# A chunked linear-attention recurrence on TensorE: state with keys on partitions, a 40-column solve, blocks inverted 16 wide and merged

## The chip, the cores and the metric

The kernel runs on one core of a Trainium2 chip. The core has TensorE (PE in the profile; its weight loads are listed apart as PEld), VectorE (DVE), ScalarE (ACT), GpSimd (POOL) and SyncE (SP), each with its own instruction queue worked in order, and 16 DMA engines that they share. The metric is the device time of one execution in microseconds, the median of several runs.

## The reference, cut to what matters

Two parts follow each other. The first is a recurrence over 768 tokens for 4 x 8 heads of width 40 (`S` in the code is the 40 x 40 state of a head):

```python
for t in range(S):
    y[:, :, t] = einsum('bhd,bhde->bhe', rt, state)
    Sa = einsum('bhde,bhe->bhd', state, at)
    state = state * wt[:, :, None, :] - einsum('bhd,bhe->bhde', Sa, bt)
    state = state + einsum('bhd,bhe->bhde', vt, kt)
```

The second is a gated mixture block over the heads' outputs `x` (768 tokens x 320):

```python
h = maximum(x @ w_in, 0)                 # 320 -> 1024
u, v = h[..., :512], h[..., 512:]
v_n = (v - mean(v)) / sqrt(var(v) + 1e-6)
v_s = einsum('ts,bsd->btd', w_spatial, v_n) + b_spatial[None, :, None]
out = (u * v_s) @ w_out                  # 512 -> 320
```

## The kernel before, in words

**Chunks.** The recurrence is worked in chunks of C = 64 tokens. A step `s` (there are 24: two pairs of batches, 12 chunks each) takes one chunk of 16 heads: 8 units `n`, each with two heads (`par` 0 and 1) on partitions 0 to 39 and 64 to 103. Within a chunk the dependence of each token on the earlier ones is a unit lower triangular 64 x 64 system. So a step is: run the decays together (two scans on VectorE, `scan1`, `scan2`, and the products `at_mul`, `sl_mul`), form the triangular matrix, invert it, and use the inverse to get all 64 updates at once.

**The inverse.** `lprime` and `lblock` put the two diagonal 32 x 32 blocks of each triangle into `Lc`. `invert(g)` takes the blocks of four chunks (a group `g`, 32 units on 128 partitions) through a 32 x 32 transpose, 30 rounds of substitution on VectorE (a product, L351, into the PSUM tile `itmp`, and a sum, L355), and two transposes back, `XT0` and `X11`. The off-diagonal block is then made on TensorE for each chunk: `b_l21`, `b_zt`, `b_x21`.

**The step's solve.** The state lies with values on partitions (`Mc`). `c_bp` multiplies it by 104 columns at once, 64 of the readout `r` and 40 of the identity; `c_ff` adds the chunk's own terms; `c_xx` applies the inverse `xf`; all three have 104 moving columns and come in two halves (`g` = 0, 1). ScalarE copies each result from PSUM (`c_bp_out`, `c_ff_out`, `c_xx_out`), GpSimd cuts the strictly triangular parts (`strict`, L396). `c_mp` updates the state, `c_y` adds to the output, `y_store` writes it to DRAM (`xs`). `b_lka` and `b_h` make two more 64 x 64 products a chunk; `b_tok` transposes two factors. The decay at a chunk's end goes through DRAM (`scr_store`, `scn_load`) to be spread over the columns of `Mc`.

**The mixture.** 12 units `j` of 128 tokens x 2 batches: load from `xs` (`m_load`), split into a high and a low part so that three products stand for one (`m_split`), four `m_u` and two `m_v` groups of eight matmuls (L742, L697), normalisation (`m_n1` to `m_n3`), results to DRAM. The weights `w_in` are decoded on VectorE and GpSimd (`decode`) in steps 4 to 10. `phase2` then does the spatial product (`spatial`, L173 to L175) and the output projection (`proj`, L193).

**Order.** Within the first phase the order on every queue is a plan written by hand: `at(t, fn, ...)` gives each piece a time in units of steps, the list is sorted, and the pieces are issued in that order. What lies beyond step 24 (the rest of the mixture) and `phase2` is ordered by the compiler's scheduler. The lines that the change touches most are these:

```python
M1, M2, M3, M4 = 0.22, 0.46, 0.65, 0.80
T_DEC, T_MOE = 4.2, 11
slots = [T_MOE + k // 4 + (M1, M2, M3, M4)[k % 4] for k in range(3 * NS)]
t0 = 2.5 if g == 1 else max(4.5, GS * g - 4 + 0.0)      # invert(g) from t0
t1 = GS * g - 1 + 0.70                                  # to t1
t = PREP.get(q, q - 8 + 0.01)                           # scans and products of chunk q
```

An fp32 matmul of this kernel is two TensorE instructions, each with a weight load of its own, so the counts in the profile are twice those in the code; transposes are one.

Of the kernel before, what the change touches and what calls it, by code (L numbers as in the profile page):

```python
# [18 lines left out]
P = 128  # L19
# [10 lines left out]
NR = C + E  # L30
LATE = 2 * C
# [180 lines left out]
def phase1(ctx, tc, early, late, vtok, win, xs, vns, uts, dscr):  # L212
    nc = tc.nc
    NS = early.shape[1]
    CPB = 12
    LO, HI = slice(0, 64), slice(64, 128)
    PR = (LO, HI)
    RR = (slice(0, E), slice(64, 64 + E))
    LV = slice(0, 64 + E)

# [15 lines left out]
    ps_b = pool("ps_b", 1, space=PSUM)  # L236
    ps_i = pool("ps_i", 1, space=PSUM)
# [24 lines left out]


# [30 lines left out]
    def scr_store(s):  # L294
        if s % CPB == 0:
            return
        sv = st["raw", s][2]
        sc = jit.tile([P, NU], F32, name="sc")
        nc.scalar.activation(sc, sv[:, :, 1], AF.Copy)
        for par in range(2):  # L300
            nc.sync.dma_start(out=scr[s, par], in_=sc[RR[par]])

    def at_mul(s, eng, ns=slice(0, NU)):
        Et, at, sl = st["pre", s]
        oth = st["raw", s][1]
        Ev = Et.rearrange("p (n c) -> p n c", c=WSEG)
        eng.tensor_tensor(out=at[:, ns], in0=oth[:, ns, 0], in1=Ev[:, ns, 0:C], op=ALU.mult)

    def sl_mul(s, eng, ns=slice(0, NU)):
        Et, at, sl = st["pre", s]  # L310
        wseg, oth, sv = st["raw", s]
        k = ns.stop - ns.start
        eng.tensor_tensor(  # L313
            out=sl[:, ns], in0=oth[:, ns, 1:],
            in1=sv[:, ns, 2:C + 2].unsqueeze(2).broadcast_to([P, k, 2, C]), op=ALU.mult,
        )

    def lprime(s):
        Et, at, sl = st["pre", s]
        pl = ps_k.tile([P, NU, HB], F32, name="bk")  # L320
        for n in range(NU):
            for blk in range(2):
                for par in range(2):
                    o = (1 - par) * 64 + blk * HB
                    cs = slice(blk * HB, (blk + 1) * HB)
                    nc.tensor.matmul(  # L326
                        pl[o:o + HB, n, :], lhsT=sl[PR[par], n, par, cs], rhs=at[PR[par], n, cs],
                        start=True, stop=True,
                    )
        st["pl", s] = pl  # L330

    def lblock(s):
        if s % GS == 0:
            st["Lc", s // GS] = inv.tile([P, GS * NU, HB], F32, name="Lc")
        Lc = st["Lc", s // GS]
        u0 = (s % GS) * NU
        nc.vector.tensor_tensor(
            out=Lc[:, u0:u0 + NU, :], in0=st.pop(("pl", s)),
            in1=maskl.unsqueeze(1).broadcast_to([P, NU, HB]), op=ALU.mult,
        )  # L340

    def invert(g):
        Lc = st.pop(("Lc", g))
        A = inv.tile([P, HB, HB], F32, name="A")
        nc.vector.transpose(out=A, in_=Lc.rearrange("p u t -> p t u"))
        yield
        nc.vector.memset(A.rearrange("p t s -> p (t s)")[:, 0:HB * HB:HB + 1], 1.0)
        for k in range(1, HB - 1):
            m = HB - 1 - k
            tp = ps_i.tile([P, m, k], F32, name="itmp")  # L350
            nc.vector.tensor_tensor(  # L351
                out=tp, in0=A[:, k + 1:, k:k + 1].broadcast_to([P, m, k]),
                in1=A[:, k:k + 1, 0:k].broadcast_to([P, m, k]), op=ALU.mult,
            )
            nc.vector.tensor_tensor(out=A[:, k + 1:, 0:k], in0=A[:, k + 1:, 0:k], in1=tp, op=ALU.add)  # L355
            yield
        XT0 = xinv.tile([P, GS * NU, HB], F32, name="XT0")
        X11 = xinv.tile([P, GS * NU, HB], F32, name="X11")
        st["X", g] = (XT0, X11)
        nc.vector.transpose(out=XT0.rearrange("p u t -> p t u"), in_=A)  # L360
        yield
        nc.vector.transpose(out=X11.rearrange("p u t -> p t u"), in_=A.rearrange("p t s -> p s t"))
        yield

    INV_N = HB + 1


    def lin_load(s):
        for par in range(2):
            nc.sync.dma_start(out=lin[s % 2][RR[par], :, 0:LATE], in_=late[par, s])  # L370

    def vtok_load(s):
        for par in range(2):
            nc.sync.dma_start(out=Rts[s % 2][par][PR[1 - par], :, C:], in_=vtok[s, par])

    def b_copy(s, par):
        if par == 0:
            At = [jat.tile([P, NU, C], F32, name=f"At{i}") for i in range(2)]
            tk = jit.tile([P, NU, 2, E], F32, name="tk")
            st["blk", s] = (At, Rts[s % 2], tk, xfs[s % 2])  # L380
# [617 lines left out]
```

## Time and profile before

| | us |
|---|---|
| three runs | 712.87, 704.87, 713.06 |
| median | 712.87 |
| span of the profiled execution | 704.4 |
| TensorE busy (matmuls) | 585.0 (83%) |
| TensorE weight loads | 529.8 (75%) |
| VectorE busy | 447.6 (64%) |
| ScalarE busy | 413.5 (59%) |
| GpSimd busy | 291.1 (41%) |

The profile is of one execution, whose time is its span and about half a microsecond around it if it is like the fastest run; no time of its own is listed for it. Rows of the timeline give the start of a run of like instructions in microseconds from the span's start, the time from its first start to its last end, the engine, the line of the kernel, the operation, the tiles (output <- input), the shape (for PE: rows*loaded columns, then partitions x moving columns) and the count. Rows of groups end in total busy time and mean nanoseconds of one, then the idle time before them and what ended it. Matmuls are pipelined: the length of one in the profile (200 to 400 ns) is its latency, and the distance between starts is what it costs.

### The profile page before, as it was taken

The page shows a single profiled execution, that of the slowest core. Times are in us where ns is not written, and L with a number is a line of the kernel's source. Part 1 is how long each engine was busy: PE and PEld are TensorE (multiplying, and loading weights), DVE is VectorE, ACT ScalarE, POOL GpSimd, SP SyncE. Part 2 cuts the span into 40 slices and gives each one's busy share as a digit, 9 for nine tenths or more (in the row PEclk, how much of TensorE's full clock was granted, in tenths as well). Part 3 has the DMA queues.
Part 4 walks back from the last instruction along what each step waited for, and adds up shares of the span by engine and source line. Part 5 has one row for each costly group of instructions (what it writes and reads, how often), then busy time and mean ns, then how long its engine had stood idle before and what let it go on. Part 6 is the DMA issues. An engine that isn't in the chain of part 4 may idle for free. (4 is left out here: it accounts for less than half of the span.)

```text
span 704.4 us, 25450 instructions
## 1 busy us (share of the span) xinstructions
PE 585.0 (83%) x10784; PEld 529.8 (75%) x10784; DVE 447.6 (64%) x884; ACT 413.5 (59%) x904; POOL 291.1 (41%) x486
## 2 busy tenths in 40 slices
PE   1706975577876778998998999999999989999997
PEld 1605865566766767987886788778889989999997
DVE  7897889977999999867789366612127521332221
ACT  2315773376555677696887789899855443331112
POOL 5101330123334455253563434545448972562221
PEclk9965897589787887799999899999999999999999
DMA  8462775284454635554547335344336464650001
GB/s 184 79 110 47 131 150 115 47 173 83 104 102 106 130 66 124 114 136 96 115 124 227 94 120 133 106 128 122 92 108 185 143 179 139 188 177 29 29 29 57
DMA packets 101337, 81.35 MB, mean 115 GB/s; under 512 B 33576, under 2 KB 90152, under 8 KB 99304
## 3 DMA queue, kind: packets, MB, share of 16 engines
q1 hardware_dynamic: 100680, 78.01, 44.7%
q10 hardware_dynamic: 544, 1.72, 1.2%
q8 instruction: 85, 1.39, 0.9%
q14 instruction: 28, 0.23, 0.1%
HBM read 59.20 MB, written 20.50 MB: 113 GB/s over the span
## 5 line engine op out<-in xcount | busy, mean ns | idle before, releaser
L396 POOL TENSOR_SCALAR_AFFINE_SELECT Rt<-Rt 64x512 f32<-64x512 f32 (+1 forms) x144 | 83.1, 579 | 97.1 <-ACT Rt L582 69.5
L545 ACT ACTIVATE Rt<-bp 64x416 f32<-64x416 f32 x96 | 49.1, 511 | 67.5 <-PE bp L535 65.8
L396 POOL TENSOR_SCALAR_AFFINE_SELECT At<-At 64x512 f32<-64x512 f32 x48 | 38.4, 801 | 93.5 <-ACT At L406 91.3
L351 DVE TENSOR_TENSOR itmp<-A 128x30 f32<-128x30 f32 (+9 forms) x180 | 74.7, 415 | 3.2
L173 PE MATMUL pg<-wsh,vh 128*128 128x384 f32 x192 | 64.8, 337 | 0.0
L174 PE MATMUL pg<-wsl,vh 128*128 128x384 f32 x192 | 64.7, 337 | 0.0
L175 PE MATMUL pg<-wsh,vl 128*128 128x384 f32 x192 | 64.6, 337 | 0.0
L355 DVE TENSOR_TENSOR A<-A,itmp 128x30 f32<-128x30 f32 (+9 forms) x180 | 59.0, 328 | 6.2
L535 PE MATMUL bp<-lin,Mc 40*64 40x104 f32 x768 | 51.6, 297 | 10.7 <-DVE y L640 10.2
L177 DVE TENSOR_TENSOR g<-pg,bb 128x384 f32<-128x384 f32 x32 | 17.8, 555 | 63.5 <-PE pg L175 58.5
L535 PEld LDWEIGHTS bp<-lin,Mc 40*64 40x64 f32 x768 | 45.2, 164 | 14.7 <-DVE y L640 12.6
L54 POOL TENSOR_TENSOR gl<-g,gh 128x384 fp32r<-128x384 f32 x32 | 33.2, 1041 | 51.1 <-ACT gh L50 50.9
L582 ACT ACTIVATE Rt<-ch 64x416 f32<-64x416 f32 x96 | 49.1, 511 | 3.9 <-PE ch L571 1.5
L326 PE MATMUL bk<-at,sl 64*32 64x32 f32 x1536 | 23.6, 215 | 30.3 <-DVE sl L313 15.2
L553 PE MATMUL ch<-Rt,At 128*64 128x104 f32 x768 | 44.9, 271 | 1.2 <-issue 1.2
L441 PE MATMUL bk<-ident,sl 128*128 128x128 f32 x192 | 31.5, 298 | 16.9 <-ACT At L406 6.8
L50 ACT ACTIVATE gh<-g 128x384 fp32r<-128x384 f32 x32 | 16.6, 522 | 48.7 <-DVE g L178 48.7
L326 PEld LDWEIGHTS bk<-at,sl 64*32 64x32 f32 x1536 | 19.7, 127 | 33.2 <-DVE sl L313 15.3
L705 DVE BATCH_NORM_STATS2 bs<-vr 128x6 f32<-128x512 f32 x24 | 16.6, 690 | 42.9 <-ACT vr L699 42.9
L571 PE MATMUL ch<-ffs,xf 64*64 64x104 f32 x768 | 43.1, 263 | 0.3 <-issue 0.3
L553 PEld LDWEIGHTS ch<-Rt,At 128*64 128x64 f32 x768 | 39.1, 147 | 5.7 <-issue 3.1
L54 POOL TENSOR_TENSOR vl<-raw,vh 128x512 fp32r<-128x512 f32 x24 | 32.1, 1348 | 25.5 <-ACT vh L50 20.6
(135 smaller groups left out, 1597.3 us busy)
## 6 DMA issues: line engine op xcount, KB each, us to landing
ein<-in_early SPq DMA_DIRECT2D x40, 387.0 KB
lin<-in_late SPq DMA_DIRECT2D x48, 160.0 KB
uts<-ur SPq DMA_DIRECT2D x48, 128.0 KB
vns<-vr SPq DMA_DIRECT2D x24, 256.0 KB
raw<-vns SPq DMA_DIRECT2D x24, 256.0 KB
ut<-uts SPq DMA_DIRECT2D x24, 256.0 KB
Rt<-in_vtok SPq DMA_DIRECT2D x48, 80.0 KB
xs<-y SPq DMA_DIRECT2D x48, 80.0 KB
```

Of the source, the lines that this page charges most:

```text
L54: eng.tensor_tensor(out=lo, in0=x, in1=hi.bitcast(F32), op=ALU.subtract)
L173: nc.tensor.matmul(pg, lhsT=vh[:, dc], rhs=w_h, start=(i == 0), stop=False)
L174: nc.tensor.matmul(pg, lhsT=vh[:, dc], rhs=w_l, start=False, stop=False)
L175: nc.tensor.matmul(pg, lhsT=vl[:, dc], rhs=w_h, start=False, stop=(i == NT - 1))
L326: nc.tensor.matmul(pl[o:o + HB, n, :], lhsT=sl[PR[par], n, par, cs], rhs=at[PR[par], n, cs], start=True, stop=True,)
L351: nc.vector.tensor_tensor(out=tp, in0=A[:, k + 1:, k:k + 1].broadcast_to([P, m, k]), in1=A[:, k:k + 1, 0:k].broadcast_to([P, m, k]), op=AL ...
L355: nc.vector.tensor_tensor(out=A[:, k + 1:, 0:k], in0=A[:, k + 1:, 0:k], in1=tp, op=ALU.add)
L396: nc.gpsimd.affine_select(out=t, in_=t, pattern=[[0, k], [1, C]], base=0, channel_multiplier=-1, compare_op=ALU.is_gt, fill=0.0,)
L535: nc.tensor.matmul(bp[PR[par], q, :], lhsT=Mc[RR[par], n, :], rhs=li[RR[par], n, C:], start=(q == 0), stop=False, skip_group_check=True,)
L545: nc.scalar.activation(Rt[par][PR[par], gp, :], st["bp", g][PR[par]], AF.Copy)
L553: nc.tensor.matmul(ff[PR[1 - par], q, :], lhsT=At[par][:, n, :], rhs=Rt[par][:, n, :], start=True, stop=True,)
L582: nc.scalar.activation(Rt[par][PR[par], gp], xx[PR[1 - par]], AF.Copy, scale=-1.0)
```

## The change

The state is kept with keys on partitions (`St`) and the solve has 40 moving columns in place of 104. `c_fv` and `c_ff` add up the right side of the solve, `c_u` applies the inverse twice, once in each orientation (`u`: tokens on partitions; and its transpose into `uvr`), `c_mp` updates `St`. The output comes from two parts: `c_ys` multiplies the state (transposed by `c_sd` into `Sd`) by `r`, and `c_gh` and `c_y` add the chunk's own terms. `c_y` runs in the next step.

`low` makes both strictly lower products of a chunk at once, with 128 loaded columns, in place of `lprime`, `b_lka` and `b_l21`. `invert` runs the substitution on 16 x 16 blocks (14 rounds, two blocks in one instruction, `itmp` in SBUF), and TensorE merges 16 to 32 (`b_y`, `b_xx`) and 32 to 64 (`b_w`, `b_x21`) for every chunk. The scans of a group's four chunks run in the first step and a half of the group before, the inversion from 1.6 to 3.2. The mixture starts at 7.4 steps in place of 11.2, the weight decode at 1.0 in place of 4.2. The decay stays on the chip (`dec_copy`).

The diff, cut to its core:

```diff
+    DEPTH = 7
+    SB = HB // 2
-    jat = pool("jat", 2)
-    linp = pool("linp")
-    etp = pool("etp", 9)
+    slp = pool("slp", 2)
+    etp = pool("etp", 8)
+    uvr = const.tile([P, NU, 4, C], F32, name="uvr")
+    itmp = const.tile([P, P], F32, name="itmp")
...
+    def low(s):
+        pt = [ps_k.tile([P, NU, C], F32, name="bk") for par in range(2)]
+        for n in range(NU):
+            for par in range(2):
+                nc.tensor.matmul(
+                    pt[par][:, n, :], lhsT=sl[RR[par], n].rearrange("p q c -> p (q c)"),
+                    rhs=at[RR[par], n, :], start=True, stop=True,
+                )
+    def lblock(s, par, eng=None):
+        for blk in range(2):
+            strict(Lc[rows, us], NU, st["tl", s][par][rows, :, cs], HB)
...
     def invert(g):
+        for k in range(1, SB - 1):
+            m = SB - 1 - k
+            tp = itmp[:, 0:2 * m * k].rearrange("p (b m k) -> p b m k", b=2, k=k)
+            nc.vector.tensor_tensor(out=tp, in0=D[:, :, k + 1:SB, k:k + 1]..., in1=D[:, :, k:k + 1, 0:k]..., op=ALU.mult)
+            nc.vector.tensor_tensor(out=D[...], in0=D[...], in1=tp, op=ALU.subtract)
...
+    def b_y(s):
+        for n in range(NU):
+            for o in range(0, P, HB):
+                nc.tensor.matmul(
+                    m4[o:o + HB, n, :], lhsT=Lc[o:o + HB, u0 + n, :], rhs=X11[o:o + HB, u0 + n, 0:SB], ...)
+    def b_xx(s):
+        for n in range(NU):
+            for o in range(0, P, HB):
+                nc.tensor.matmul(m5[o:o + HB, 0, n, :], lhsT=wy[o:o + HB, n, :], rhs=XT0[o:o + HB, u0 + n, SB:], ...)
+        for n in range(NU):
+            for o in (0, 64):
+                nc.tensor.matmul(m5[o:o + HB, 1, n, :], lhsT=XT0[o:o + HB, u0 + n, :], rhs=wy[o:o + HB, n, 0:SB], ...)
+            for o in (0, 64):
+                nc.tensor.matmul(m5[o:o + HB, 1, n, :], lhsT=ident[...], rhs=X11[o:o + HB, u0 + n, 0:SB], ...)
+    def b_w(s):
+                nc.tensor.matmul(m2[o:o + 64, n, :], lhsT=tl[par][o:o + HB, n, :], rhs=X11[o:o + HB, u0 + n, :], ...)
     def b_x21(s):
+                nc.tensor.matmul(m3[o:o + 64, n, :], lhsT=wi[o + HB:o + 64, n, :], rhs=XT0[o + HB:o + 64, u0 + n, :], ...)
     def b_xcopy(s):
+            nc.sync.dma_start(out=xfs[s % 2][o:o + HB, :, 0:HB], in_=XT0[o:o + HB, us])
...
+    def c_fv(s, g):
+                nc.tensor.matmul(ff[PR[1 - par], q, :], lhsT=tl[par][PR[par], n, :], rhs=Rt[par][PR[par], n, :], ...)
     def c_ff(s, g):
+                nc.tensor.matmul(st["ff", g][PR[1 - par], q, :], lhsT=at[RR[par], n, :], rhs=Sv[RR[par], n, :], ...)
+    def c_u(s, g):
+                nc.tensor.matmul(u[PR[par], q, 0:E], lhsT=xf[ev, n, :], rhs=ffs[ev, q * E:(q + 1) * E], ...)
+                nc.tensor.matmul(u[PR[par], q, E:], lhsT=ffs[ev, q * E:q * E + C], rhs=xf[ev, n, :], ...)
     def c_mp(s, g):
+                nc.tensor.matmul(st["ff", g][RR[par], q, :], lhsT=tk[:, n, par, :], rhs=Rt[par][:, n, :], ...)
+    def c_sd(s):
+                nc.tensor.matmul(sd[PR[par], n, :], lhsT=St[RR[par], n * E:n * E + C], rhs=ident[RR[par], RR[par]], ...)
+    def c_ys(s):
+                nc.tensor.matmul(yb[PR[par], n, :], lhsT=Sd[RR[par], n * E:n * E + C], rhs=uvr[RR[par], n, 3, :], ...)
+    def c_gh(s):
+                nc.tensor.matmul(gh[par][:, n, :], lhsT=uvr[RR[par], n, par:2 + par, :]..., rhs=uvr[RR[par], n, 3, :], ...)
     def c_y(s):
+                nc.tensor.matmul(yb[RR[par], n, :], lhsT=tk[:, n, par, :], rhs=ghs[par][:, n, :], ...)
...
+            at(s + 0.00 + 0.02 * g, c_fv, s, g)
+            at(s + 0.01 + 0.02 * g, c_ff, s, g)
+            at(s + 0.20 + 0.05 * g, c_u, s, g)
+            at(s + 0.36 + 0.05 * g, c_mp, s, g)
+        at(s + 0.06, c_sd, s)
+        at(s + 0.62, c_ys, s)
+        at(s + 0.50, c_gh, s)
+        ty = s + (1.12 if s < NS - 1 else 0.80)
+        at(ty, c_y, s)
+        at(b + 0.30, b_y, q)
+        at(b + 0.46, b_xx, q)
+        at(b + 0.47, b_xcopy, q)
+        at(b + 0.64, b_w, q)
+        at(b + 0.76, b_x21, q)
+        at(b + 0.64, uvr_load, q)
+    PREP = (0.05, 0.40, 0.75, 1.10)
+        t = GS * (q // GS) - GS + PREP[q % GS]
+        t0 = GS * g - GS + PREP[3] + 0.50
+        t1 = GS * g - 0.80
+    T_DEC, T_MOE, D_DEC = 1.0, 7.4, 0.9
+        t0 = max(2 * j + 3.28, T_MOE + 1.5 * j)
+        gap = 1 / 3 if t0 + 2 < NS else 0.2
```

More of the change, by code (lines that the diff above doesn't have):

```diff
@@ L292, in scan2, with dec_copy, at_mul @@
         )
-    def scr_store(s):
+    def dec_copy(s):
         if s % CPB == 0:
             return
[L297 to L303, printed above, removed]
+        dec = etp.tile([P, NU], F32, name="dec")
+        act_copy(dec, st["raw", s][2][:, :, 1])
+        st["dk", s] = dec
+    def at_mul(s):
         Et, at, sl = st["pre", s]
@@ L332, in lblock @@
[L332 to L380, printed above, removed]
-        at = st["pre", s][1]
-        nc.scalar.activation(st["blk", s][0][par][PR[par]], at[PR[par]], AF.Copy)
@@ L384, in b_lka @@
-    def b_lka(s):
-        Et, at, sl = st["pre", s]
-        pk = ps_k.tile([P, NU, C], F32, name="bk")
+        pt = [ps_k.tile([P, NU, C], F32, name="bk") for par in range(2)]
         for n in range(NU):
@@ new lines, in vtok_load @@
+    def vtok_load(s):
+        for par in range(2):
+            nc.sync.dma_start(out=Rts[s % 2][par][PR[par]], in_=vtok[s, par])
+    def b_w(s):
+        XT0, X11 = st["X", s // GS]
+        u0 = (s % GS) * NU
+        tl = st["tl", s]
+        m2 = ps_k.tile([P, NU, HB], F32, name="bk")
+        for n in range(NU):
+            for par in range(2):
+                o = 64 - 64 * par
+                nc.tensor.matmul(
+                    m2[o:o + 64, n, :], lhsT=tl[par][o:o + HB, n, :],
+                    rhs=X11[o:o + HB, u0 + n, :], start=True, stop=True,
@@ new lines, in c_gh_out, with c_y @@
+    def c_gh_out(s, par):
+        if par == 0:
+            st["ghs", s] = [jit.tile([P, NU, C], F32, name=f"ghs{i}") for i in range(2)]
+        act_copy(st["ghs", s][par], st["gh", s][par])
+        for rows in PR:
+            strict(st["ghs", s][par][rows], NU)
+    def c_y(s):
+        tk, ghs, yb = st["tk", s], st["ghs", s], st["yb", s]
+        for n in range(NU):
+            for par in range(2):
+                nc.tensor.matmul(
+                    yb[RR[par], n, :], lhsT=tk[:, n, par, :], rhs=ghs[par][:, n, :],
+                    start=(first(s) and n == 0), stop=True, skip_group_check=True,
+                )
@@ L634, in c_y_out @@
+    def c_y_out(s):
         c = s % CPB
```

617 lines of the change are left out of this document (289 added, 328 removed).

## The prediction

> **What bounds the kernel now.** I read the page's engine shares and 40 slices first, then busy time by stage (columns: stretch; its length; PE, PEld, DVE, ACT, POOL busy us; granted clock).
>
> ```profile
> span 704.4 us, 25450 instructions
> ...
> PE   1706975577876778998998999999999989999997
> ...
> DVE  7897889977999999867789366612127521332221
> ```
>
> ```profile
> 74.10:284.00 209.90, 154.45 (x4214) 138.56 (x4204) 191.09 (x361) 129.88 (x289) 76.34 (x94) 0.83 0.54 111
> 284.00:518.40 234.40, 219.44 (x4653) 190.12 (x4641) 136.90 (x301) 195.62 (x427) 111.69 (x223) 0.97 0.45 122
> 518.40:704.40 186.00, 179.51 (x1162) 172.79 (x1160) 59.81 (x113) 63.48 (x134) 86.00 (x131) 1.00 0.37 116
> ```
>
> Three regimes. Up to about 284 us VectorE is the bound (191 of 210 us busy; the granted clock is only 0.83, as PE waits). From 284 PE is (219 of 234), and still in the tail (180 of 186). So a saving on VectorE pays only in the first 284 us; whatever the change adds on PE is paid in full after it.
>
> **What a PE block costs.** Timeline rows of warm blocks (start, from first start to last end, count; an fp32 product is two matmuls, two products on separate parts of the array alternate):
>
> ```profile
> 324.26 0.76 PE L326 MATMUL bk<-at,sl 64*32 64x32 f32 x64
> ...
> 421.22 0.63 PE L742 MATMUL pv<-xh,wh 128*128 128x256 f32 x3
> ...
> 422.37 1.09 PE L627 MATMUL bp<-Rt,tk 128*40 128x64 f32 x32
> ```
>
> ```profile
> 426.96 1.65 PE L553 MATMUL ch<-Rt,At 128*64 128x104 f32 x32
> ...
> 428.54 0.66 PE L441 MATMUL bk<-ident,sl 128*128 128x128 f32 x4
> ...
> 429.79 0.95 PE L697 MATMUL pv<-wh,xh 128*128 128x512 f32 x3
> ...
> 431.81 0.70 PE L458 MATMUL bk<-sl,at 64*32 64x32 f32 x32
> ...
> 435.77 1.15 PE L419 MATMUL bk<-lin 40*64 40x64 f32 x32
> 436.85 0.51 PE L603 MATMUL ch<-tk,Rt 128*40 128x40 f32 x16
> ...
> 438.59 0.69 PE L504 MATMUL bk<-zt,X 32*32 32x32 f32 x32 [0.28 <-ACT zt L486]
> ```
>
> The distance from L553 to the next block is 1.58 us, from L419 1.08; with 0.15 of turnover that is 0.089 a pair at 104 moving columns and 0.058 at 64. L419's length then leaves some 0.23 for its last matmul's own latency; taken off the others it gives about 0.03 a pair at 32 columns (L504), 0.037 at 40 (L603) and 0.034 for each four of L326. I use 0.088, 0.059, 0.038, 0.032 and 0.034, with 0.15 turnover per block, and 0.11 for a transpose.
>
> These shapes all have as many loaded columns as moving ones, or fewer. The change turns that round: 64 loaded and 40 moving, 128 and 64, 64 and 32, 32 and 16. So the weight load's own time decides. The same query cut a moment later shows it (PEld; columns as above):
>
> ```profile
> 426.96 0.14 PEld L553 LDWEIGHTS ch<-Rt,At 128*64 128x64 f32 x2
> 426.96 0.20 PEld L553 LDWEIGHTS ch<-Rt,At 128*64 128x64 f32 x4
> 429.76 0.19 PEld L697 LDWEIGHTS pv<-wh,xh 128*128 128x128 f32 x1
> 429.76 0.30 PEld L697 LDWEIGHTS pv<-wh,xh 128*128 128x128 f32 x2
> 429.76 0.54 PEld L697 LDWEIGHTS pv<-wh,xh 128*128 128x128 f32 x3
> 428.54 0.20 PEld L441 LDWEIGHTS bk<-ident,sl 128*128 128x128 f32 x2
> ```
>
> The second load on each of L553's two array parts ends 0.06 after the first (64 columns); L697's second 0.11 after the first (128). The third comes 0.24 later, when a 512-column matmul has let go: one load is held ready, not two. So a pair cannot be faster than its load: I take 0.059 for 64 loaded columns however few move, 0.112 for 128, 0.032 for 32. L441, a transpose, loads 128 columns in 0.06; that is the low end for the 128-column blocks.
>
> **The step, before and after** (PE us).
>
> Before: lprime 0.7; b_lka, b_h and c_y 1.08 each; the three 32-wide blocks 0.65 each; c_bp, c_ff, c_xx 16 x 0.088 + 0.15 = 1.56 each; transposes 1.0; c_mp 0.9. Sum 12.5.
>
> After: low 16 x 0.112 + 0.15 = 1.94; transposes 1.0; b_y 0.7; b_xx 0.58 + 32 x 0.032 + 0.15 = 1.75; b_w and b_x21 (64 loaded) 1.09 each; c_fv and c_ff 32 x 0.059 + 0.3 = 2.19; c_sd 1.09; c_u 2.19; c_mp 0.9; c_gh 1.94; c_ys and c_y 1.09 each. Sum 18.1: the solve is narrower, but its pairs wait for 64-column loads, and b_y, b_xx and the wide blocks are added.
>
> Over the run: low and transposes for 20 chunks (four lie in the start) 20 x 2.96 = 59; merging for 23 chunks 23 x 4.65 = 107; the step itself 24 x 10.5 = 252, less 8 where a batch starts or ends. Together **410 us**.
>
> A rule of the Trainium skill speaks against narrowing as such: "TensorEngine Tiling (Array Packing)", Instruction Overhead, says a matmul of one moving column takes as long as one of 60. The rows disagree (0.032 a pair at 32 columns, 0.059 at 64). By the rule b_y and b_xx would cost an estimated 1.7 us more a step, 38 in all.
>
> Stalls come on top. One late step:
>
> ```profile
> 423.61:441.53 17.92, 16.93 (x360) 14.77 (x360) 11.81 (x29) 16.39 (x35) 8.60 (x17) 1.00 0.49 131
> ```
>
> Its blocks, without lprime 11.8, and three L742 groups (421.22 to 422.37: 1.15) and one L697 group (429.79 to 431.81: 2.02) sum to 17.3, so 0.65 was stall; the stretch 284 to 518 (12 steps, 8 mixture units of 4 x 1.15 + 2 x 2.02 = 8.64) leaves 1.5 a step. I take 1.1: 24 x 1.1 = **26**. The new merge adds two PE-ACT-PE turns a step, but the plan puts other blocks between.
>
> **VectorE.** Rows (last columns: busy us, mean ns):
>
> ```profile
> L351 DVE TENSOR_TENSOR itmp<-A 128x30 f32<-128x30 f32 (+9 forms) x180 | 74.7, 415 | 3.2
> L355 DVE TENSOR_TENSOR A<-A,itmp 128x30 f32<-128x30 f32 (+9 forms) x180 | 59.0, 328 | 6.2
> L345 DVE STREAM_TRANSPOSE A<-Lc 128x1024 f32<-128x1024 f32 x6 | 11.8, 1961 | 0.2
> L281 DVE TENSOR_TENSOR_SCAN S<-ein,ends 128x528 f32<-128x528 f32 x24 | 30.3, 1263 | 1.1 <-DMA ein<-in_early 1.1
> L313 DVE TENSOR_TENSOR sl<-ein,S 128x1024 f32<-128x1024 f32 x24 | 33.7, 1405 | 0.0
> L617 DVE TENSOR_TENSOR Mc<-mn,scn 104x160 f32<-104x160 f32 x44 | 22.4, 508 | 1.4
> L640 DVE TENSOR_TENSOR y<-bp,Et 104x256 f32<-104x256 f32 x48 | 19.9, 419 | 24.0 <-PE bp L627 23.9
> L382 ACT ACTIVATE At<-at 64x512 f32<-64x512 f32 x48 | 30.2, 629 | 0.9
> 0.00:740.00 740.00, 42.33 (x70) 5.65 (x10) 27.24 (x20) 0.91 0.45 110
> ```
>
> Substitution goes from 60 instructions a group (22.3 us) to 28 of 28 to 112 elements; between
>
> ```profile
> 52.28 0.27 DVE L355 TENSOR_TENSOR A<-A,itmp 128x108 f32<-128x108 f32 x1
> ...
> 53.88 0.19 DVE L355 TENSOR_TENSOR A<-A,itmp 128x30 f32<-128x30 f32 x1
> ```
>
> that is about 0.27 each with its gap: 7.6, with three transposes (5.9) and memsets 14 instead of 28. A step then has 5.1 of scans and products (L281, L313 and two between them), 3.5 of inversion, 2.2 of state and output (about two L617, two sums and two L640) and, in steps 1 to 6.4, 5.5 of weight decode (the last row is the decode's tiles over the span: 42.3 us, some 30 of it for these weights): 16.3, below PE's 19.2. So VectorE stops being the bound, and its 14 us a group buy only what PE leaves.
>
> **What is costed at nothing.** ScalarE loses six copies of 64x512 (L382: 0.63) and eight of 64x416, gains fewer and smaller ones, and has spare time in every step; uncovered it would add no more than the two turns above. POOL has ten selects a step instead of eight, needed half a step later; c_y alone waits for the last four, about 3 us, and lies 0.6 of a step behind them. The copy of the diagonal block goes from ScalarE to SP, 0.7 of a step ahead of its reader. One wait is new there: the load of r and v for the next step waits for c_ys of this one, because that tile is single now; behind it on SP stand the output store and the next loads, whose readers are most of a step away. The decay's store and broadcast load leave SP (88 transfers). The mixture's loads and stores move four steps forward past the decode's, into a stretch where the DMA engines are half busy (0.54 in the first stage row). If SP's order did stall PE, it would be a transfer's 2 to 3 us in some steps: under 20 in all, inside the range.
>
> **The start.**
>
> ```profile
> 25.04 1.11 PE L441 MATMUL bk<-ident,sl 128*128 128x128 f32 x4
> ...
> 29.64 1.96 DVE L345 STREAM_TRANSPOSE A<-Lc 128x1024 f32<-128x1024 f32 x1
> ...
> 55.87 1.92 DVE L362 STREAM_TRANSPOSE X<-A 128x1024 f32<-128x1024 f32 x1
> ...
> 62.58 1.06 PE L458 MATMUL bk<-sl,at 64*32 64x32 f32 x32
> 63.58 3.04 PE L571 MATMUL ch<-ffs,xf 64*64 64x104 f32 x32
> ```
>
> The first inversion runs alone, 29.64 to 57.8, and the first solve starts at 63.6. PE is cold here (L458's block 1.06, not 0.70). Per chunk PE now has low (about 3.3 cold), two transpose blocks of 1.1 and evictions between, some 6.6 us against VectorE's 5.1, so the fourth chunk's blocks reach POOL late and the inversion starts near 37. It takes 14, and then four merges in series, cold, about 10: **61** to the first solve (54 if PE warms, 66 if not). Of the 14 us saved, some 3 remain.
>
> **Sum.** 61 + 410 + 26 + mixture 12 x 8.64 = 104 + second phase 147 (the last stretch's 186, less 4 units, 35, and 5 for the rest of a step) + 2 for the seam, where spatial weights now wait for buffers of steps 21 to 23: **750** against the profiled 704.4. Starting the mixture at step 7 moves PE work forward into a PE-bound stretch: nothing is gained. The three runs were 704.87, 712.87 and 713.06; the profiled one agrees with the fastest, so against the median 712.9 this is +5%. One measurement cannot tell 2% (14 us) from no change.
>
> **Rivals.**
> 1. *Loads stay hidden*: pairs go by moving columns. low, c_gh 1.09; b_w, b_x21 0.66; c_fv with c_ff 1.5; c_sd 0.76; c_u 1.85: 14.3 a step, 322 in all, 88 less; VectorE's 16.3 then binds in steps 1 to 6, +7: **669**, clearly faster. Against it: one load is held ready. For it: no row has more loaded than moving columns. It decides if a 64/40 pair takes under 0.05. Chance 0.12.
> 2. *Only 128-column loads are quick* (0.06, as L441's): low and c_gh 1.09: 750 - 44 x 0.85 = **713**. Chance 0.07.
> 3. *Row halves don't run side by side*: low and c_gh use rows 0-39 and 64-103 but all 128 columns; no row shows that. If serial, 32 x 0.107: +1.6 for each of 44 blocks: **822**. Chance 0.12. The Trainium skill, "TensorE: Matmul & The Clock Gate", The mechanism, says loads overlap running matmuls only when row groups differ, which low and c_gh meet; by it the sum stays 750. L553's rows disagree in part: its loads overlap with all 128 rows in use.
> 4. *Queue stalls*: ps_k turns nine tiles a step through two buffers, PE waits on ACT 2 us a step: 772. Within the forecast's own spread of 725 to 775.
>
> **Numbers.** Forecast 0.66 (its lower tail to 725), rivals 1 to 3 0.31, others 0.03. Range 705 to 822: it leaves out rival 1 and half of rival 3. Faster by over 2% (below 698.6): rival 1 and a bit, 0.15. Within 2% (to 727): rival 2 and the forecast's edge, 0.14. Slower 0.71.
>
> **What would show it.** PE 95% busy in all steps, VectorE below 85% before 200 us; steps near 19 us without mixture and 25 with it; blocks of 32 with 64 loaded and 40 moving columns 1.1 long, those of low and c_gh 2.0; the first solve near 61. If c_fv's 16 matmuls take 0.5 from start to end instead of 0.7, rival 1 holds and I am wrong.

## The result: 931.4 us, 1.32 times the time before

The changed kernel takes a median of 931.43 us (929.42 to 942.86, four runs) beside 709.85 for the kernel before (704.87 to 713.06): a ratio of 1.317, 95% interval 1.307 to 1.327. The forecast was 750, range 705 to 822: the sign is right, the size is not. The profiled execution took 929.42, its span 927.7.

From the page of the changed kernel (engine totals, then slices; PEclk is the granted clock in tenths):

```profile
span 927.7 us, 33760 instructions
...
PE 850.1 (92%) x15200; PEld 788.6 (85%) x15200; DVE 344.1 (37%) x646; ACT 298.6 (32%) x760; POOL 338.6 (36%) x534
...
PE   4579799999999998999999999999999787999998
...
DVE  7444515464442522243523244523111431423221
...
PEclk9999856756566685778877779667977697999999
```

And by stage (stretch; length; busy time of PE, PEld, DVE, ACT, POOL; granted clock; DMA share, GB/s), with the first stretch of the kernel before and the totals of its page ahead:

```profile
0.00:74.10 74.10, 31.58 (x796) 28.29 (x800) 59.82 (x110) 24.51 (x55) 17.04 (x38) 0.78 0.56 106
```

```profile
PE 585.0 (83%) x10784; PEld 529.8 (75%) x10784; DVE 447.6 (64%) x884; ACT 413.5 (59%) x904; POOL 291.1 (41%) x486
```

```profile
0.00:74.10 74.10, 45.91 (x738) 42.23 (x740) 42.57 (x71) 18.11 (x47) 28.20 (x48) 1.00 0.49 97
74.10:284.00 209.90, 196.56 (x4194) 184.66 (x4192) 97.77 (x180) 60.72 (x167) 72.37 (x92) 0.68 0.31 68
284.00:518.40 234.40, 226.20 (x4550) 204.76 (x4550) 81.59 (x161) 83.29 (x221) 86.58 (x154) 0.74 0.35 83
518.40:766.00 247.60, 228.25 (x4842) 204.98 (x4830) 79.84 (x165) 90.17 (x235) 82.17 (x170) 0.77 0.32 89
766.00:927.70 161.70, 153.21 (x912) 151.99 (x912) 42.33 (x70) 46.31 (x92) 69.25 (x72) 0.96 0.33 104
```

VectorE went from 191 busy microseconds in the second stretch to 98, and PE from 154 to 197 of 210: PE is the bound from step 1 on, as forecast. What was not forecast stands in the clock column: 0.68, 0.74 and 0.77 where PE is 92 to 97% busy. Every clock record is 0.5 or 1.0, so a mean of 0.74 over 234 us is 2 x 0.26 x 234 = 122 us at half clock. Over the run the records give 379 us at half clock, before the change 126. (The first record is at 103.8 us, before the change at 34.0; until then the page shows 1.00, but the pitches are those of half clock. The half-clock times of the runs below are those of the records alone. The first record comes at 19 to 103.8 us, depending on the run, so small differences between these times mean little.)

The 223 us between the two spans can be split. PE's busy time (the time in which the trace has a matmul running), with half weight where the records say 0.5 and before the first of them, is its work at full clock: 531 us before, 636 after. The rest of its busy time is lost to the clock: 54 before, 214 after. What is left of the span is PE's idle time: 119 and 78. So 223 = **104 of work, 161 of clock, 42 less idle**. With the clock loss of before, and all else equal, the span would have been 767.

### The profile page after: what moved, and what is told of

Read it like the earlier page. It is cut to its first block, busy times and chain, and to the rows that moved or that the text cites. A ratio compares the mean times of both kernels' runs of the same rounds, so it can differ in the third digit from the quotient of the medians.

```text
span 927.7 us, 33760 instructions
## 1 busy us (share of the span) xinstructions
PE 850.1 (92%) x15200; PEld 788.6 (85%) x15200; DVE 344.1 (37%) x646; ACT 298.6 (32%) x760; POOL 338.6 (36%) x534
## 4 chain that ended last, share of the span: by engine, by line
PE 88%; issue 3%; ACT 3%; DMA 2%; DVE 2%; SPq 1%; POOL 0%; ACTq 0%; DVEq 0%; POOLq 0%
PE bk L328 7%; PE pv L713 7%; PE ch L625 7%; PE pv L758 6%; PE po L191 5%; PE bk L495 4%; PE bk L363 4%; PE ff L517 4%; PE bk L474 4%; PE yb L643 4%; PE pg L171 4%; PE pg L172 4%; PE pg L173 4%; PE yb L616 4%; PE ch L545 3%
## 5 line engine op out<-in xcount | busy, mean ns | idle before, releaser
L340 POOL TENSOR_SCALAR_AFFINE_SELECT Lc<-tl 32x256 f32<-32x256 f32 x96 | 62.4, 650 | 148.7 <-ACT tl L270 136.1
L340 POOL TENSOR_SCALAR_AFFINE_SELECT ghs<-ghs 64x512 f32<-64x512 f32 x96 | 67.5, 703 | 117.4 <-ACT ghs L270 113.1
L328 PE MATMUL bk<-at,sl 40*128 40x64 f32 x768 | 74.3, 339 | 13.2 <-DVE sl L318 11.4
L328 PEld LDWEIGHTS bk<-at,sl 40*128 40x128 f32 x768 | 68.6, 247 | 17.8 <-DVE sl L318 11.4
L625 PE MATMUL ch<-uvr 40*128 40x64 f32 x768 | 66.6, 337 | 3.1 <-issue 3.1
L625 PEld LDWEIGHTS ch<-uvr 40*128 40x128 f32 x768 | 62.4, 246 | 4.5 <-issue 3.7
L495 PE MATMUL bk<-XT,wi 32*64 32x32 f32 x768 | 41.5, 274 | 12.3 <-ACT wi L270 11.4
L495 PEld LDWEIGHTS bk<-XT,wi 32*64 32x64 f32 x768 | 38.4, 199 | 16.1 <-ACT wi L270 12.8
L517 PE MATMUL ff<-Rt,tl 64*64 64x40 f32 x768 | 44.5, 281 | 0.0
L270 ACT ACTIVATE Rt<-ch 64x160 f32<-64x160 f32 x96 | 28.6, 298 | 47.8 <-PE ch L552 46.4
L340 POOL TENSOR_SCALAR_AFFINE_SELECT tl<-tl 64x512 f32<-64x512 f32 x48 | 42.6, 888 | 2.7
```

Source lines behind the costliest of these rows:

```text
L270: nc.scalar.activation(out, in_, AF.Copy)
L328: nc.tensor.matmul(pt[par][:, n, :], lhsT=sl[RR[par], n].rearrange("p q c -> p (q c)"), rhs=at[RR[par], n, :], start=True, stop=True,)
L340: nc.gpsimd.affine_select(out=t, in_=t if src is None else src, pattern=[[0, k], [1, w]], base=0, channel_multiplier=-1, compare_op=ALU.is ...
L495: nc.tensor.matmul(m3[o:o + 64, n, :], lhsT=wi[o + HB:o + 64, n, :], rhs=XT0[o + HB:o + 64, u0 + n, :], start=True, stop=True,)
L517: nc.tensor.matmul(ff[PR[1 - par], q, :], lhsT=tl[par][PR[par], n, :], rhs=Rt[par][PR[par], n, :], start=(q == 0), stop=first(s), skip_gro ...
L625: nc.tensor.matmul(gh[par][:, n, :], lhsT=uvr[RR[par], n, par:2 + par, :].rearrange("p q c -> p (q c)"), rhs=uvr[RR[par], n, 3, :], start= ...
```

## What a block costs at each clock

Timeline rows of the changed kernel (start, from first start to last end, line, count). The clock is 1.0 from 274.5 to 281.3, from 298.4 on for a while and in the last two rows, and 0.5 from 281.3 to 298.4:

```profile
277.03 0.70 PE L428 MATMUL bk<-XT,wy 32*32 32x16 f32 x62
...
279.23 2.00 PE L625 MATMUL ch<-uvr 40*128 40x64 f32 x32
281.17 1.88 PE L616 MATMUL yb<-uvr,Sd 40*64 40x64 f32 x32
282.97 1.91 PE L474 MATMUL bk<-X,tl 32*64 32x32 f32 x32
...
286.82 1.92 PE L495 MATMUL bk<-XT,wi 32*64 32x32 f32 x32
...
298.80 0.66 PE L545 MATMUL ch<-ffs,xf 64*64 64x40 f32 x16
299.29 0.66 PE L552 MATMUL ch<-xf,ffs 64*64 64x64 f32 x16
...
527.52 1.15 PE L616 MATMUL yb<-uvr,Sd 40*64 40x64 f32 x32
528.60 1.12 PE L474 MATMUL bk<-X,tl 32*64 32x32 f32 x32
```

c_gh (L625) is 2.0 long, as forecast for 128 loaded columns. c_u's half (L545) is followed by the next block after 0.49 us: 0.06 a pair with 64 loaded and 40 moving, and the same with 64 moving (L552). So the load does decide, as the forecast said. But c_ys (L616), b_w (L474) and b_x21 (L495) take 1.9 us at 0.5, where 1.09 was forecast; at 1.0 they take 1.1. Busy times from 274.5 to 281.3 and from 281.3 to 298.4 (columns as above):

```profile
274.50:281.30 6.80, 6.42 (x268) 5.97 (x262) 4.61 (x9) 2.17 (x9) 0.00 (x0) 1.00 0.20 53
281.30:298.40 17.10, 17.10 (x230) 15.32 (x230) 1.15 (x2) 3.73 (x9) 2.99 (x4) 0.50 0.44 100
```

In the second PE is busy for 17.10 of 17.10 us, at half clock. Waiting can't be what keeps the clock down here.

## Experiments: what lets the clock drop

Three theories were tried first. A: the clock follows the time in which columns are moved, which a load-bound block fills only in part. B: it follows the part of the array in use. C: it follows waits and gaps between blocks. Where columns are moved the whole time, a matmul of 512 columns follows the last after 0.43 us in m1, 0.84 ns a column.

**Blocks by themselves** (m1). `blocks(rows, loaded, moving)` on two or four parts of the array, nothing waits.

> This kernel leaves the whole computation out: it runs one kind of matmul block at a time, back to back and with no waits, for about 25 us each, every stretch after some 9 us of 128x128 products of 512 columns; then the sequence of blocks of one changed step four times without waits, once as it is and once with the moving side widened to the loaded width (40 to 64, 32 to 64, 64 to 128). Theory A (the clock follows the columns that are moved: a block that waits for its loads moves for only half of the time and lets the clock drop): the stretches with fewer moving than loaded columns (64 loaded and 40 moving, 128 and 64, 64 and 32) fall to a granted clock of 0.5 after one or two windows, 0.10 to 0.11 us a pair for 64 loaded and 0.21 for 128; the same with as many moving as loaded stay at 1.0, 0.059 and 0.112 a pair; the plain step sequence comes out near 0.7, the widened one at 1.0 and shorter in spite of more columns. Theory B (it follows the part of the array in use): all stretches with 32 or 40 rows fall to 0.5 whatever they move, those with 64 and 128 rows on both halves stay at 1.0; widening changes nothing. Theory C (it follows waits and gaps between blocks): every stretch here and both sequences stay at 1.0, since nothing waits.

Windows of some stretches (columns: stretch, length, PE, PEld, ACT, POOL, clock, DMA). In order: 64 rows with 64 loaded and 40 moving; 40 rows with 128 and 64; 40 rows with 128 and 128; 32 rows with 64 and 32; 32 rows with 64 and 64:

```profile
23.40:70.00 46.60, 46.60 (x1599) 46.60 (x1598) 0.00 (x0) 0.00 (x0) 1.00 0.02 4
134.50:225.90 91.40, 91.40 (x856) 91.39 (x856) 0.00 (x0) 0.00 (x0) 0.51 0.01 1
236.50:285.60 49.10, 49.10 (x879) 49.10 (x880) 0.00 (x0) 0.00 (x0) 1.00 0.01 2
294.60:377.50 82.90, 82.90 (x1599) 82.89 (x1600) 0.00 (x0) 0.00 (x0) 0.52 0.01 3
389.00:435.70 46.70, 46.70 (x1601) 46.68 (x1600) 0.00 (x0) 0.00 (x0) 1.00 0.02 4
```

C falls: PE is busy without a break in all of these, and two fall to half clock. B in its plain form falls: 40 and 32 rows hold the clock when as many columns move as are loaded. A misses one of its own: 64 rows with 40 of 64 moving stay at 1.0. The pitches agree with the forecast: 46.6 us over 800 pairs is 0.058 a pair at 40 and at 64 moving. (Two stretches of 32x32 blocks fell too, but with gaps: PE was busy for 46 of 90 us in the first, so they tell nothing apart. The last part, a step's blocks in order, came out in another order than written and is not used.)

**The widened kernels** (e2, e3, e4). The results are the same; more columns are moved. The edits are cut here: the last unit, which has no neighbour, stays narrow in some blocks, and e4 also widens the merges' 16 columns to 32.

```
-    ff[PR[1 - par], q, :], ..., rhs=Rt[par][PR[par], n, :]                 # 40 moving
+    ff[PR[1 - par], q, 0:64], ..., rhs=Rt_flat[PR[par], n * E:n * E + C]   # 64 moving (e2: also c_ff, c_sd, c_u, b_w, b_x21)
-    pt[par][:, n, :], ..., rhs=at[RR[par], n, :]                           # 64 moving
+    pt[par][:, n:n + 2, :], ..., rhs=at[RR[par], n:n + 2, :]               # 128 moving (e3: also c_gh)
```

> The changed kernel, but the blocks that load 64 columns and move 40 or 32 (the right side from v, from the state and the transposed state, the solve's state side, the two wide merges) move 64: the columns beyond are a neighbour's and are not read. It computes the same. Theory A (the pairs are bound by their loads, and the clock drops where a block moves too few columns for the time its loads take): no block gets longer at the same clock (0.059 a pair at 1.0), and the time at 0.5, 379 of 928 us, goes down by a third or more: 930 becomes 790 to 870. Theory C (waits and gaps between blocks lower the clock): clock and time as before, 920 to 940. Theory D (load and move add up, or it is the work that counts): 24 columns more on 88 products a step add some 88 x 0.02 us x 24 = 40 us: 970.

> The changed kernel, but low and c_gh, which load 128 columns and move 64, move 128 (this unit's and the next one's; the next product overwrites the second half). It computes the same. Theory A: 0.112 a pair at clock 1.0 as before, the time at 0.5 goes down by a quarter: 930 becomes 820 to 890. Theory C: 920 to 940. Theory D: twice the moving columns on 32 products a step add 32 x 0.05 us x 24 = 40 us: 970.

> Both widenings together, and the 16-column products of the merges moved 32 wide as well, as wide as what they load. It computes the same, with some 60% more moving columns in the recurrence. Theory A: the granted clock is 0.95 or more through the steps, under 60 us of the span at 0.5, and the time comes to what the pitches at full clock gave, 740 to 780. Theory C: 920 to 940. Theory D: 1000 or more.

Measured: e2 904.62 (two executions, 894.72 and 914.52; half-clock time 331 us), e3 907.10 (898.01 and 916.19; 303), e4 841.49 (830.97 to 850.30; ratio to before 1.172, 1.162 to 1.181; 188). All lie below the changed kernel's 929.42 to 942.86. Moving more columns made the kernel 90 us faster, which no theory in which the work or the waits count allows; but A's ranges were missed as well: e2 and e3 gained less than it said, and e4 did not reach 780.

**Thresholds** (m2), and a better measure.

> Leaves the whole computation out. Stretches of one block kind, back to back without waits, from a warm clock and from a cold one (a stretch of 128 loaded and 32 moving goes ahead). With the share of its time in which a part of the array moves columns as the measure (columns x 2 / 2.4 GHz over the pair's pitch at full clock), 64 loaded columns give 0.51 at 36 moving, 0.46 at 32, 0.40 at 28, 0.57 at 40, 0.68 at 48, 0.80 at 56, 0.91 at 64; 128 loaded on one part 0.48 at 32 and 0.60 at 40, twice that of the halves since one part takes every load. Theory A (the share sets the clock, with one threshold to fall and a higher one to rise, as the windows of the changed kernel suggest: no fall above 0.5, no rise below 0.75): from warm, 32 and fewer fall to 0.5 and 36 is at the edge; from cold, 40 and 48 stay at 0.5, 56 and 64 rise. Theory A' (one threshold of 0.5 both ways): 40 and 48 rise too. Theory C (waits): every stretch is at 1.0 within two windows.

In order: 64 rows, 64 loaded, from a warm clock with 28 and 24 moving; from a cold one with 40 and 48:

```profile
135.30:181.90 46.60, 46.60 (x1599) 46.60 (x1600) 0.00 (x0) 0.00 (x0) 1.00 0.02 5
192.60:272.80 80.20, 80.20 (x1599) 80.20 (x1600) 0.00 (x0) 0.00 (x0) 0.54 0.01 3
300.50:385.70 85.20, 85.20 (x1600) 85.20 (x1600) 0.00 (x0) 0.00 (x0) 0.50 0.01 2
413.40:461.70 48.30, 48.30 (x1602) 48.28 (x1600) 0.00 (x0) 0.00 (x0) 0.96 0.02 4
```

28 of 64 holds and 24 falls; from cold 40 stays down and 48 rises. So there are two edges, as A said, but it had both wrong by a step: 36, 32 and 28 hold, where 32 and fewer were to fall, and 48 rises, where it was to stay. 64 rows hold the clock at 0.40 of the time, while in m1 40 rows lost it at 0.48. The rows have to be counted.

**Row share** is the rows in use out of 128, times moving columns over loaded ones (where fewer move than are loaded). The stretches give, with the pairs' own pitch: 0.40 held and 0.35 lost with 64 rows a half; 0.30 (40 rows, 128 and 64) and 0.23 (32 rows, 64 and 32) lost; 0.46 (32 rows, 64 and 64) held. Counting cells, that is rows times loaded columns, does not order them: 64 rows with 64 loaded and 28 moving feed 0.20 of the array's cells and hold, 40 rows with 128 and 64 feed 0.30 and lose. On one part with all 128 rows and 128 loaded columns, 40 moving (row share 0.31) lose the clock from warm, and 64 (0.50) do not bring it back from cold.

The same can be worked out for each 3.41 us window of a kernel's trace: each matmul's columns times 0.84 ns (half of that in the mixture, twice at half clock), times its rows over 128, or times a half for two blocks side by side that share all rows; each matmul counts in the window in which it starts. Over the eleven full kernels of this study, of the windows at 1.0 with a share under 0.36, 219 of 227 were followed by half clock; over 0.40, 2 of 1432. Of those at 0.5 under 0.70, 4 of 455 were followed by full clock; over 0.80, 171 of 187. With the one edge that suits it best, the row share is wrong on 26 of all 1723 windows at 1.0; the time in which columns move on 71, the cells fed on 100, PE's busy share on 151.

**Rows alone** (e8), then with the wide columns (e9). No instruction, wait, load or moved column is added in the loop in e8; shown is `low`, and c_gh, c_ff, c_sd and c_ys are changed likewise.

```
-    ..., lhsT=sl[RR[par], n]..., rhs=at[RR[par], n, :]     # rows 0-39 and 64-103
+    ..., lhsT=sl[PR[par], n]..., rhs=at[PR[par], n, :]     # rows 0-63 and 64-127; 40-63 are zero on one side
```

> The changed kernel, but low, c_gh, c_ff, c_sd and c_ys, which use 40 rows of each half of the array, use 64: rows 40 to 63 of one side are zero. It computes the same; loaded and moved columns, instructions and waits are unchanged. Theory R (what sets the clock is the share of the array's rows that are fed with moving columns, averaged over 3.4 us: in the traces so far windows above 0.40 hardly ever lose the clock, windows below 0.36 mostly do, and it comes back after a window above 0.75): these five blocks' share goes up by 64/40 (low and c_gh from 0.30 to 0.48, above the edge), so half-clock time falls from 379 us to 200 to 280 and 930 becomes 840 to 885. Theory A (the share of time that the parts move, rows not counted): nothing changes, 915 to 945.

> The widest version (64 or 128 columns moved wherever as many are loaded, 32 in the merges) with the 64 rows as well. Theory R: the half-clock time falls from 188 us to under 110, 841 becomes 785 to 810; at full clock throughout the sum would be 750. Theory A: as with the wide columns alone, 830 to 850.

Measured: e8 886.29 (868.25 to 901.20), just above the 840 to 885 of R, with more half-clock time than R said (304 us), and below all that A allowed; e9 788.11 (779.74 to 793.18), ratio to before 1.105 (1.098 to 1.112), as R said. The executions of these kernels differ by up to 4%, and their granted clocks with them (0.842 in e8's fastest, 0.831 in its slowest). Slices of e4, then of e9:

```profile
PE   4759899989999979999899999999995959999998
...
PEclk9998967769669598998999998799968979999999
```

```profile
span 791.4 us, 33762 instructions
...
PE   4468888898898899999999999899986699999997
...
PEclk9859998999999989999999999999996989999999
```

With 85 us at half clock instead of 379, e9 is 143 us faster than the changed kernel although it moves far more columns and uses more rows for the same results. The split of the span shows where the time went (us, of the profiled executions, worked out as above):

| | span | work at full clock | lost to the clock | idle |
|---|---|---|---|---|
| before | 704 | 531 | 54 | 119 |
| changed | 928 | 636 | 214 | 78 |
| e2, 64 wide | 893 | 643 | 172 | 78 |
| e8, 64 rows | 888 | 645 | 160 | 83 |
| e4, all wide | 845 | 655 | 103 | 86 |
| e9, both | 791 | 665 | 32 | 94 |

From the changed kernel to e9 work and idle time grow a little, and only the loss to the clock shrinks, by some 182 us.

**The measures against each other** (m3), from shapes in which they part.

> Leaves the whole computation out. Stretches of one block kind again, from a warm clock and from a cold one, chosen so that the two measures part. Row share: rows in use of the 128, times the share of the time in which they are fed with moving columns; time share: the latter alone. From warm, 128 loaded and 64 moving (time share 0.48): with 64 rows of each half row share 0.48, with 56 rows 0.42, with 40 rows 0.30; 32 rows, 64 loaded, 48 moving: time share 0.68, row share 0.34; 56 moving: 0.80 and 0.40; all rows, 128 loaded and 56 moving: 0.44 in both. From cold: 128 loaded and 128 moving with 64 rows 1.0 in both, with 40 rows 1.0 and 0.62; 32 rows with 64 loaded and 64 moving 1.0 and 0.5. Theory R (row share: falls below about 0.36 to 0.40, rises above about 0.75): from warm the 64-row, the 56-row and the all-row stretch hold at 1.0, the 40-row one and 32 rows with 48 moving fall to 0.5, 56 moving is at the edge; from cold only 64 rows rise. Theory A (time share, same edges): all hold from warm and all rise from cold.

```profile
20.70:69.80 49.10, 49.10 (x879) 49.07 (x880) 0.00 (x0) 0.00 (x0) 1.00 0.01 2
140.30:229.40 89.10, 89.10 (x879) 89.10 (x880) 0.00 (x0) 0.00 (x0) 0.53 0.01 1
242.40:323.30 80.90, 80.90 (x1601) 80.90 (x1600) 0.00 (x0) 0.00 (x0) 0.53 0.01 3
335.30:382.20 46.90, 46.90 (x1601) 46.80 (x1600) 0.00 (x0) 0.00 (x0) 1.00 0.02 4
481.30:530.50 49.20, 49.20 (x881) 49.18 (x880) 0.60 (x1) 0.00 (x0) 1.00 0.08 18
555.00:648.90 93.90, 93.90 (x880) 93.87 (x880) 0.00 (x0) 0.00 (x0) 0.50 0.00 1
676.80:762.10 85.30, 85.30 (x1600) 85.26 (x1600) 0.00 (x0) 0.00 (x0) 0.50 0.01 2
```

From warm: 64 rows with 128 loaded and 64 moving hold (low, as e8 has it); 40 rows fall (low as the change has it); 32 rows fall with 48 of 64 moving and hold with 56. From cold, with as many moving as loaded: 64 rows rise, 40 and 32 rows stay at half clock for the whole 94 and 85 us. Every stretch went as the row share said (56 moving it had put at the edge), and four of these seven against the time share; the two that aren't shown, 56 rows and all rows, hold, as both measures had it.

## Experiments: the parts of the change

**The mixture at step 11** (e5): `T_DEC, T_MOE, D_DEC = 1.0, 11.0, 0.9` instead of 7.4.

> The changed kernel with the mixture's first unit at step 11 instead of 7, as before the change. Theory A: the early steps lose the mixture's 128x256 and 128x512 blocks, which move columns nearly all the time and lift the clock; more of the steps 7 to 11 at 0.5, and 2 to 3 units more lie in the tail at full clock: 925 to 955. If the early start had been what costs: 880 to 910.

952.20 (two executions, 938.49 and 965.90), half-clock time 436 us. The early start is not what cost: nothing comes near 880 to 910. That it helped is not shown: the faster execution lies within the changed kernel's 929.42 to 942.86, and with the time before the first record (66.1 us here, 103.8 there) the loss to the clock is 225 us beside 214.

**The substitution alone**: in the kernel before, the 16-wide substitution with b_y and b_xx, in the first three groups (e6) or in all (e7); the four chunks of a group are merged within 1.1 steps after the inversion, since the blocks' tile is needed again. State, solve and mixture are as before.

```
+        if g in G16:            # e6: groups 0 to 2, e7: all
+            ... 28 instructions of two 16-wide blocks instead of 60
+        if q // GS in G16:
+            at(tm, b_y, q); at(tm + 0.01, b_y_out, q); at(tm + 0.14, b_xx, q); at(tm + 0.15, b_xx_out, q)
```

> The kernel before the change with the 16-wide substitution and TensorE's merges put in for the first three groups alone (chunks 0 to 11, whose inversions lie in the stretch where VectorE was the bound); state, solve and mixture stay as before. Substitution 14 instead of 28 us a group: the start shortens by 14 less some 4 for the first merge, and two more groups give VectorE 14 us each in its stretch: 28 of it if nothing else binds there, 10 if PE, at a clock below 1 by then, takes over. 710 becomes 670 to 690 (Theory A: the merges' blocks are short and the solve's 104 columns a product keep the clock up). Rival: the merges' 32x32 blocks lower the clock in the steps as they did after the change, and PE's own 10 us a group come at half clock: 710 to 725.

> The same in all six groups: this part of the change alone. In the groups 3 to 5 PE is the bound, so the merges' 2.5 us a chunk come on top: 12 x 2.5 = 30 us more than with three groups, less what VectorE's relief gives in group 3: 690 to 715. So of the change's loss of 220 us this part would carry none. Rival: it carries a good part of it through the clock, 760 or more.

Both expectations of e6 missed, and e7's main one; e7's rival holds. e6 takes 738.05, ratio 1.045 (1.036 to 1.053); e7 792.02, ratio 1.120 (1.113 to 1.127). The second stretch of e6, and the totals of e7's page:

```profile
74.10:284.00 209.90, 167.99 (x5352) 151.94 (x5348) 139.08 (x252) 122.62 (x289) 65.50 (x79) 0.77 0.45 98
```

```profile
PE 679.5 (86%) x15392; PEld 619.8 (79%) x15392; DVE 367.5 (47%) x698; ACT 440.7 (56%) x1004; POOL 291.0 (37%) x493
```

VectorE is at 139 of 210 instead of 191, and nothing else is full, yet the stretch gets through fewer steps, not more. Taken step by step, the reason shows. Four steps, the fourth to the seventh, each from the end of one chunk's last sum into `y` (L640) to the end of the next one's, first of the kernel before, then of e6 (columns as in the stage rows above):

```profile
113.30:142.80 29.50, 16.52 (x420) 14.93 (x418) 28.20 (x60) 12.24 (x27) 4.30 (x8) 0.67 0.30 66
142.80:163.00 20.20, 16.23 (x487) 14.75 (x484) 13.71 (x29) 13.24 (x29) 4.64 (x8) 0.84 0.88 172
163.00:184.80 21.80, 15.72 (x427) 13.53 (x416) 19.90 (x40) 13.25 (x30) 9.14 (x10) 0.89 0.35 82
184.80:205.90 21.10, 15.59 (x390) 14.20 (x392) 20.55 (x41) 12.81 (x29) 9.72 (x10) 0.82 0.59 122
```

```profile
122.90:155.80 32.90, 26.76 (x876) 24.57 (x876) 17.48 (x29) 15.30 (x38) 5.39 (x8) 0.60 0.32 64
155.80:186.70 30.90, 25.19 (x822) 22.76 (x816) 13.05 (x28) 14.32 (x34) 5.61 (x9) 0.67 0.52 108
186.70:204.10 17.40, 13.77 (x392) 12.28 (x388) 16.22 (x32) 13.03 (x29) 8.32 (x10) 0.90 0.40 107
204.10:221.00 16.90, 12.78 (x404) 11.31 (x395) 16.37 (x32) 12.92 (x29) 8.53 (x10) 1.00 0.61 154
```

In the last two, which hold no merge, VectorE's relief did shorten the step, by 4.4 and 4.2 us. The first two hold the group's four merges, at a clock of 0.60 and 0.67, and are 3.4 and 10.7 us longer; the next group's merges make two more steps 10.1 and 4.5 longer, and the first chunk comes out 9.5 us later. So the relief was real, and the merges, crowded as they are here, cost more than it gave. Split as above, e7's 84 us are 52 of PE work, 43 of clock and 11 less idle; e6's 29 are 27, 15 and 12 less. How much of the change's own 223 us is this part's does not follow: the change spreads the merges, one chunk a step, and that was not tried in the kernel before.

**The rows in the kernel before** (e10): b_h and c_bp with 64 rows.

```
-    lhsT=Mc[RR[par], n, :], rhs=li[RR[par], n, C:]
+    lhsT=Mc[PR[par], n, :], rhs=li[PR[par], n, C:]
```

> The kernel before the change with 64 rows instead of 40 (rows 40 to 63 zero) in b_h and c_bp, the two blocks of its step that use 40. Theory R: the half-clock time, 126 us, nearly all before 320 us, falls a little (to 90 to 120), since waits and not these blocks cause most of it; the time goes down by 0 to 8 us. Rival: where VectorE ends the waits PE's clock does not matter, and the time stays within 0.5%.

705.71 beside 711.17, ratio 0.994 (0.991 to 0.998): a small gain that costs no instruction in the loop. It is what R said, but the interval reaches into the rival's 0.5%, so this run does not decide between them. Half-clock time is 107 us instead of 126. Its second stretch has 145.45 busy microseconds of PE instead of 154.45, at 0.85 instead of 0.83:

```profile
74.10:284.00 209.90, 145.45 (x4067) 130.68 (x4067) 187.26 (x353) 128.80 (x287) 74.98 (x93) 0.85 0.54 109
```

## Why the prediction was right in sign and wrong in size

**The step that failed** is that every pitch of the sum after the start was taken at full clock: the loss to the clock in the steps is a term put at nothing. The reason was the remark in the first part, "the granted clock is only 0.83, as PE waits": as PE was to be 95% busy, the clock was to be full. For the kernel before the remark is right: in the 16 windows of 3.4 us after which its clock fell, PE was busy for a third of the time on average, and for 78% at most. What failed is to carry it over. In the changed kernel PE was busy for 78% on average in the 27 windows before a fall, and all the time in two of them. All rows for the pitches came from after 324 us, where the clock was 0.97 to 1.00 in a mix of 104-column products and the mixture's 128 rows.

The changed blocks have row shares (rows over 128, times moving over loaded columns) of 0.31 (low, c_gh), 0.25 (b_w, b_x21), 0.39 (c_ff, c_sd), 0.5 or less (b_y, b_xx) and 0.62 (c_fv, c_ys, the first half of c_u): the first four lie below the edge at which the clock falls, the next two at it, and none reaches the 0.75 from which it comes back. Only transposes, c_mp, c_y, the half of c_u that moves 64, and the mixture do. That cost 161 us more than before the change, shown by e4, e8 and e9 to go with the row share and not with work or waits. The trace of before could not show it: of its windows at full clock with a share under 0.36, 14 of 15 lost it, and of 140 above 0.40 none, but in those that lost it PE was waiting too.

**The sign** was not luck. Work at full clock grew by 104 us, because blocks are added and their pairs wait for their loads, as forecast, and even e9, which loses less to the clock than the kernel before, is some 10% slower than it. **The pitches** held at full clock: 0.058 a pair where 64 columns are loaded, 2.00 us for c_gh, 1.12 for b_w. b_xx, from 277.03 to 279.23, takes 2.2 where 1.75 was summed, with a gap of 0.38 in it; where no gap falls in, it takes 1.65. With no clock loss after the first 60 us, the span would be 729, if nothing else came to bind; with the loss of before, 767. So apart from the clock the sum came out 21 us too high, and that it is no more is partly chance: the stalls, taken at 1.1 a step although the prediction's own stretch had left 1.5, came to 1.6 (PE was idle for 36 us in the 23 steps from 102.4 to 759.8), and other terms made up for them.

**Rivals 1 and 2** (loads hidden) are refuted by the pitch of 0.058 with 40 moving and 0.112 with 128 loaded (49.10 us for 440 pairs in m3). **Rival 3** (row halves one after the other) by the same row: serial they would take 0.21 each. **Rival 4** (queues, 2 us a step) is not ruled out by much, with 1.6 us of PE's idle time a step from all causes, but it could explain only some 12 of the 178 us between 750 and the profiled span. None of the rivals had the clock.

**The start** came as worked out. VectorE and PE rows of the changed kernel:

```profile
37.11 1.93 DVE L380 STREAM_TRANSPOSE A<-Lc 128x1024 f32<-128x1024 f32 x1 [11.15 <-POOL Lc L340]
...
49.09 1.92 DVE L403 STREAM_TRANSPOSE XT<-A 128x1024 f32<-128x1024 f32 x1
```

```profile
60.06 1.93 PE L517 MATMUL ff<-Rt,tl 64*64 64x40 f32 x32
```

The inversion runs from 37.1 to 51.0 (forecast 37, 14 long), the first solve starts at 60.1 (61, or 66 if PE did not warm, and it did not). What was missed is that PE stays at half clock until 103.8.

**The seam** was put at 2 us, for buffers of steps 21 to 23; the longest wait there is another, for the split of the last mixture unit:

```profile
769.51 0.79 PE L758 MATMUL pv<-xh,wh 128*128 128x256 f32 x2 [7.56 <-ACT xh L48]
```

**Steps** were to be 19 us without mixture and 25 with it; from the first output at 102.4 to the last at 759.8, 23 steps took 28.6 on average, and 23.5 in e9.

**The rule weighed there**, the Trainium skill's "TensorEngine Tiling (Array Packing)", Instruction Overhead, by which b_y and b_xx would take an estimated 1.7 us more a step, isn't borne out: at full clock and without a gap b_xx came out at 1.65 beside the 1.75 of the sum, and b_y at 0.66 beside 0.7.

## What to carry to other kernels

A busy TensorE is not a fast one: before pitches are added up, work out for each block the rows in use out of 128 times moving over loaded columns, and, by these runs, expect half clock where it averages under 0.36 to 0.40 over 3.4 us, and no return below about 0.75. Narrowing these fp32 products below their loaded width saved nothing on TensorE and cost the clock; where rows or columns are free to be padded with zeros or with a neighbour's, padding them is worth trying. And judge the relief of a full engine step by step: in e6 it shortened the steps without merges by a fifth, and the steps that took the added work lost more than that.

## What the runs showed of the hardware

The granted clock knew only 0.5 and 1.0, and its spells, but for the last, cut off by the end, were multiples of 3.4 us. It fell with PE busy for every nanosecond of a stretch, and stayed at half clock for 94 us of gapless work at 40 rows. The Trainium skill, "TensorE: Matmul & The Clock Gate", Part 1 (What's actually happening), says that a monitor sets the clock to half or full by how busy PE has been, in windows of 3.4 us: windows and values agree with these traces, "busy" has to be read as the share of rows that are being fed, with two edges, near 0.36 to 0.40 and near 0.75. That page puts the fall down to idle gaps (HAM oscillation); the stretches above have none. Columns in use do not count as rows do: by cells fed, 0.20 held and 0.30 lost. How rows are counted where two blocks share all 128 of them was not tried by itself; a half each fits the windows best.
